# A fused attention and gated-MLP kernel with its Gelu in three stages in place of four (two segments share one stage, two are read from PSUM) and with new scheduling rules

## The chip, the cores and the metric

The kernel runs on one core of one Trainium2 chip. The metric is the device time of one launch in microseconds (us). The kernel before took 312.73 us (median of 3 runs, 310.44 to 313.6) when the prediction was made. The profile is one execution on that core; its span runs from the first to the last instruction and is 1 to 2 us shorter than the time of the same run.

## The reference, cut to what matters

Two branches read the same `x` (2048 tokens, 512 channels) and are mixed by a gate per token. Branch A works in four segments of 512 tokens with 32 heads of width 16: softmax attention inside the segment, plus a linear memory `M, z` that is carried from segment to segment. Branch B is a gated MLP with 1792 hidden channels.

```
for s in range(4):                       # segments of 512 tokens
    p = softmax(q_s k_s^T * scale + mask); a_dot = p v_s
    a_mem = (phi(q_s) M) / (phi(q_s) z + 1e-6)      # phi(t) = t+1 if t>0 else exp(t)
    o_s = g * a_mem + (1 - g) * a_dot
    M += phi(k_s)^T v_s ;  z += sum phi(k_s)
a = concat(o_s) @ wo
b = (gelu(x @ w_gate) * (x @ w_up)) @ w_down
out = sigmoid(x . gate_w) * a + (1 - that) * b
```

Exp and Gelu both run on ScalarE, and the traces show a table load of 1.28 us there at each change from one to the other, so the order of the two on ScalarE matters.

## The kernel before

The kernel is written as tasks with estimated durations; when it is built, a list scheduler in Python puts them in one fixed order per engine. So "the kernel" is a task graph, a set of picking rules, and the order that falls out of them. Every engine is given its own fixed order, with semaphores to wait on in it.

The kernel uses eight banks of PSUM, the memory that its matmuls write to. Four (`X`) hold one fill of attention scores, one (`P`) the result of the probabilities times the values (called PV here), and three (`W`) serve all other matmuls. One exp reads all four score banks at once.

```
# the pick (cut)
for e in ENGINES:
    for t in ready[e]:
        st = max(cur[e], ready_at[t.id])
        if t.tiled == "pv":
            ...                                  # PV goes right after a score fill, else
            st += PATIENCE                       # it is held back by 3 us
        if t.grp is not None and t.grp.bank is None:
            if not bank_free: continue
            st = max(st, min(bank_free.values()))
        k = (st, -t.prio, t.id)
        if best is None or k < best[0]: best = (k, e, t)
```

```
# one fill (cut): scores into X[0..3], one exp of 128x2048, masks on GpSimd;
# five fills and two PVs per group of 8 heads, 20 fills per segment, 80 in all
exp: activation(PT[slot], XALL, Exp, scale=ATT_SCALE)

def gates(s):      # hidden tile ft: 4 matmuls into a W bank, copied out by ScalarE or VectorE
    copy_out(f"Gev{s}_{ft}", g, hT[s%2][:, ft, :], g.f32(), ..., engs=(ACT, DVE))
def gelu(s):       # 14 tiles in 4 chunks, SBUF to SBUF, after all exps of phase s
    ... after=exp_tasks[s] + previous chunk
def ups_down(s):   # 14 x 4 up matmuls, multiplied into hT by VectorE, then 4 tiles of
    ...            # wo (4 matmuls) + wd (14 matmuls), in pieces of 3, attention part first
    ostage[tile % 2] = psum * omgt               # ScalarE or VectorE; two output buffers

prep(0)
for s in range(4):
    attention(s)
    prep(s + 1)            # K, Q, V, gate, phi(q), memory read; phi(k) and memory update
    gates(s); gl = gelu(s); ups_down(s, gl)
```

`prep(s+1)` runs in phase `s`, under the exps of the segment ahead. `hT` has two slots, so hidden states of two segments can be held.

The softmax here doesn't subtract the row's maximum and nothing guards it: scores larger than these inputs give would overflow.

Of the kernel before, what the change touches and what calls it, by code (L numbers as in the profile page):

```python
# [12 lines left out]
ALU = mybir.AluOpType  # L13
# [13 lines left out]
PATIENCE = 3.0  # L27
HOP = {PE: 0.17, ACT: 0.07, DVE: 0.07, POOL: 0.10, SP: 0.0}
# [40 lines left out]
class Task:  # L69


    def __init__(self, name, alts, grp=None, after=(), bias=0.0, nbytes=0):
# [6 lines left out]
        self.tiled = None  # L79
        self.est = {e: sum(i.est for i in l) for e, l in alts.items()}  # L80
# [13 lines left out]
class Sched:  # L94
# [32 lines left out]
    def schedule(self):  # L127
# [6 lines left out]
        for g in groups.values():  # L134
            for t in g[1:]:
                for d in t.preds:
                    if d.grp is not g[0].grp and d is not g[0]:
                        if d not in g[0].preds:
                            g[0].preds.add(d)
                            d.succs.add(g[0])  # L140
# [23 lines left out]
        while len(order) < n:  # L164
            best = None
            for e in ENGINES:
                for t in ready[e]:
                    st = max(cur[e], ready_at[t.id])
                    if t.tiled == "pv":
                        if last_pe == "qk" and ready_at[t.id] <= cur[e]:  # L170
                            best = ((-1.0, 0.0, t.id), e, t)
                            continue
                        st += PATIENCE
# [4 lines left out]
                    k = (st, -t.prio, t.id)  # L178
# [150 lines left out]
def _build(es, nc, A_x, A_wq, A_wk, A_wv, A_wo, A_beta, B_w_gate, B_w_up, B_w_down, gate_w, out):  # L329
# [41 lines left out]
    ostage = [sb(f"ost{i}", [P, 512]) for i in range(2)]  # L371
# [149 lines left out]
    gelu_last = [None] * NSEG  # L521

# [45 lines left out]
    def prep(s):  # L568
# [51 lines left out]
        if s > 0:  # L620
# [14 lines left out]
            for qt in range(4):  # L635
# [14 lines left out]
                    issue=1.25, transpose=True)  # L650
        if s < NSEG - 1:
            for i in range(2):
                phi_task("pk", s, ph, kT, "kT", kT, "kT", i)
# [27 lines left out]
    def attention(s):  # L681
        sl = s % 2
        for t in range(4):
            slots = {}

            def fill(name, steps, diags):
# [4 lines left out]
                for (j, kb, ncol, c0) in steps:  # L691
                    for g in range(4):
# [4 lines left out]
                            [("kpad", j, sl, t), ("qT", sl, t)], [("X", g)], 0.4 * ncol / 512 / 4))  # L697
                task(f"qk{s}_{t}{name}", PE, instrs).tiled = "qk"
# [3 lines left out]
                    [("X", g) for g in range(4)], [("PT", slot)], act_t(2048))], after=after)  # L702
                minstrs = []
# [13 lines left out]
            def pv(j, sa, sbk, sc):  # L717
                i2 = t % 2
                instrs = []
                for kb in range(4):  # L720
                    slot, c0 = ((sa, 0), (sbk, 0), (sc, 256 * j), (sbk, 384))[kb]
                    for q in range(4):
# [5 lines left out]
                            [("PT", slot), ("Vaug", sl, kb)], [("P",)], 0.04))  # L728
                task(f"pv{s}_{t}_{j}", PE, instrs).tiled = "pv"
# [3 lines left out]
            def norm():  # L733
# [9 lines left out]
                          [("recip", i2)], 0.25),  # L743
                    Instr(lambda e: e.tensor_tensor(sc1[i2][:], recip[i2][:], gd, ALU.mult),
                          [("recip", i2), ("GdT", sl)], [("sc1", i2)], 0.2),
                    Instr(lambda e: e.tensor_tensor(ov, tv[:, :, :, 0:16], rb, ALU.mult),  # L746
                          [("Tb", i2, 0), ("Tb", i2, 1), ("sc1", i2)], [("obf", i2)], dve_t(512)),
                    Instr(lambda e: e.transpose(dst, obf[i2][:]), [("obf", i2)], dk, dve_t(512))]  # L748
                if s > 0:
                    ins.append(Instr(lambda e, t=t: e.tensor_tensor(oT[sl][:, t, :], oT[sl][:, t, :], ott[i2][:],  # L750
                                                                    ALU.add), ok + dk, ok, dve_t(512, 2)))
# [11 lines left out]
    CHUNKS = [(0, 2), (2, 6), (6, 10), (10, 14)]  # L763

    def gates(s):
        sl, x3 = s % 2, s % NX
        for ft in range(NFT):
            g = Grp(banks)
            pieces(f"G{s}_{ft}", g, [mm(g, lambda g=g: g.f32()[:, :], wg[:, kb, ft * 128:(ft + 1) * 128],
                                        xT[x3][:, kb, :], [("xT", x3, kb), ("w", ("wg", ft // 7))], kb == 0,  # L770
                                        kb == 3, 512) for kb in range(4)], 2)
            copy_out(f"Gev{s}_{ft}", g, lambda ft=ft: hT[sl][:, ft, :], lambda g=g: g.f32()[:, :], [g.key],
                     [("hT", sl, ft)], 512)

    def gelu(s):
        sl = s % 2
        res = []
        for ci, (f0, f1) in enumerate(CHUNKS):
            hk = [("hT", sl, ft) for ft in range(f0, f1)]
            res.append(task(f"gelu{s}_{ci}", ACT, [Instr(  # L780
                lambda e, f0=f0, f1=f1: e.activation(hT[sl][:, f0:f1, :], hT[sl][:, f0:f1, :],  # L781
# [124 lines left out]
```

## Time and profile before

| | before |
|---|---|
| time, us | 312.73 |
| span of the profiled run, us | 309.8 |
| TensorE / VectorE / ScalarE busy | 90% / 65% / 71% |
| TensorE idle in the span, us | 30.0 |
| 80 exps of 128x2048, each | 1.877 us |
| a warm matmul of 512 columns, one after another | 0.2165 us |

The page's first part has busy time, share of the span and instruction count of each engine:

```profile
PE 279.8 (90%) x2185; PEld 114.1 (37%) x2185; DVE 202.1 (65%) x352; ACT 218.8 (71%) x163; POOL 104.4 (34%) x193
```

The span was cut at the starts of exps number 0, 19, 20, 39, 40, 59, 60 and 79 (counted from 0). The stretch ahead of the first exp (15.4 us) is left out. Rows 1, 3, 5 and 7 are stretches of 19 rounds of "scores, exp", rows 2, 4 and 6 hold a last exp of a phase and the Gelu stage behind it, and the last row runs from the last exp to the end. Columns of the windows view, kernel before: stretch and length; busy time and instruction count of TensorE, weight loads, VectorE, ScalarE and GpSimd; then the granted TensorE clock, the DMA share and GB/s.

```profile
...
15.41:72.87 57.46, 50.30 (x446) 19.59 (x448) 44.91 (x87) 47.72 (x43) 26.64 (x58) 0.97 0.42 117
72.87:84.80 11.93, 11.47 (x95) 5.76 (x88) 10.34 (x18) 11.87 (x9) 1.28 (x2) 1.00 0.22 44
84.80:140.31 55.51, 49.54 (x431) 19.35 (x433) 42.30 (x77) 41.13 (x28) 23.46 (x42) 0.97 0.14 25
140.31:151.27 10.96, 10.96 (x76) 5.21 (x69) 5.07 (x8) 10.90 (x7) 1.27 (x2) 1.00 0.24 48
151.27:206.23 54.96, 50.86 (x443) 20.27 (x444) 42.09 (x71) 42.19 (x31) 23.28 (x42) 1.00 0.02 6
206.23:217.19 10.96, 10.49 (x86) 4.89 (x79) 6.56 (x11) 10.90 (x7) 1.27 (x2) 1.00 0.13 36
217.19:271.33 54.14, 51.91 (x426) 20.26 (x428) 32.59 (x53) 38.02 (x24) 20.02 (x26) 1.00 0.08 19
271.33:309.80 38.47, 33.29 (x177) 14.17 (x169) 16.49 (x26) 11.68 (x9) 1.27 (x2) 1.00 0.06 21
```

The timeline of ScalarE shows the first Gelu stage of before. Columns: start, duration, engine, source line, operation, out<-in and count:

```profile
72.87 1.88 ACT L700 ACTIVATE pt<-psXALL 128x2048 bf16<-128x2048 f32 x1 [0.33 <-PE psXALL L693]
...
75.26 1.28 ACT L781 ACT_TABLE_LOAD   x1
76.55 4.66 ACT L781 ACTIVATE hT<-hT 128x1024 bf16<-128x1024 bf16 x3
...
83.51 1.28 ACT L700 ACT_TABLE_LOAD   x1
84.80 1.88 ACT L700 ACTIVATE pt<-psXALL 128x2048 bf16<-128x2048 f32 x1
```

And the timeline of TensorE at the end of before (L402 is the helper that emits all `W` matmuls):

```profile
275.40 12.75 PE L402 MATMUL psW<-xT,wu 128*128 128x512 bf16 x56
...
288.74 1.47 PE L402 MATMUL psW<-wo,oT 128*128 128x512 bf16 x6
292.27 0.39 PE L402 MATMUL psW<-wo,oT 128*128 128x512 bf16 x1 [2.07 <-DVE oT L750]
...
300.91 5.78 PE L402 MATMUL psW<-wd,hT 128*128 128x512 bf16 x26
```

After the last exp all ups and downs of the last segment are still to do, and one wait of 2.07 us falls among them: the attention part of the down tile needs the last normalised output (`oT`), which VectorE is only just finishing.

### The profile page before, as it was taken

What the parts mean: (1) busy time and instruction counts of PE and PEld (TensorE: products, weight loads), DVE (VectorE), ACT (ScalarE), POOL (GpSimd) and SP (SyncE); (2) the same over time, 40 slices, a digit from 0 to 9 for tenths busy, and PEclk for the clock granted to TensorE, in tenths of its full rate; (3) what the DMA queues carried; (4) which work ended last, traced back from release to release, by engine and by line L of the source; (5) the groups of instructions that cost most, each with busy time, mean ns of one, the idle gap of its engine ahead of it and who ended that gap; (6) DMA issues with size and microseconds to landing.
All of it is one profiled execution on the core that took longest, in us unless ns stands there. A gap on an engine that the chain in (4) does not pass through costs nothing.

```text
span 309.8 us, 5374 instructions
## 1 busy us (share of the span) xinstructions
PE 279.8 (90%) x2185; PEld 114.1 (37%) x2185; DVE 202.1 (65%) x352; ACT 218.8 (71%) x163; POOL 104.4 (34%) x193
## 2 busy tenths in 40 slices
PE   5999779979976997999989997989998999999795
PEld 1434223334422333444424333434432433344242
DVE  0176799688888977394796767846668274657600
ACT  1399679678996876579989867769866677793000
POOL 7036434732033834332065433330334243410000
PEclk9599979999997999999999999999999999999999
DMA  6999600022200000633100000001400000000000
GB/s 202 260 360 300 119 19 0 2 47 47 45 2 0 2 0 1 87 87 67 37 0 2 0 0 2 1 2 51 72 18 2 0 19 17 2 34 0 2 34 34
DMA packets 29769, 15.30 MB, mean 49 GB/s; under 512 B 21296, under 2 KB 29744, under 8 KB 29744
## 3 DMA queue, kind: packets, MB, share of 16 engines
q1 hardware_dynamic: 28160, 13.91, 17.9%
q10 hardware_dynamic: 1584, 1.05, 1.1%
q8 instruction: 17, 0.28, 0.4%
q14 instruction: 8, 0.07, 0.1%
HBM read 8.14 MB, written 2.10 MB: 33 GB/s over the span
## 4 chain that ended last, share of the span: by engine, by line
PE 59%; DVE 18%; SPq 8%; ACT 8%; issue 3%; DMA 2%; POOL 2%; ACTq 0%; DVEq 0%; POOLq 0%
PE psW L402 48%; PE psXALL L693 6%; PE psP L724 5%; ACT pt L700 4%; SPq L433 4%; SPq L429 3%; DVE obf L746 3%; DMA betaT<-in_A_beta_dram 2%; DVE tb L730 2%; DVE oT L750 2%; DVE ott L748 2%; ACT hT L781 2%; DVE hT L419 1%; POOL exsT L611 1%; DVE hT L796 1%
## 5 line engine op out<-in xcount | busy, mean ns | idle before, releaser
L700 ACT ACTIVATE pt<-psXALL 128x2048 bf16<-128x2048 f32 x80 | 150.1, 1877 | 47.3 <-PE psXALL L693 38.9
L711 POOL TENSOR_SCALAR_AFFINE_SELECT pt<-pt 128x512 bf16<-128x512 bf16 (+1 forms) x112 | 83.0, 743 | 165.2 <-ACT pt L700 155.7
L402 PE MATMUL psW<-xT,wg 128*128 128x512 bf16 x224 | 56.3, 386 | 5.3 <-DVE hT L419 3.4
L402 PE MATMUL psW<-xT,wu 128*128 128x512 bf16 x224 | 53.6, 380 | 3.2 <-DVE hT L796 3.1
L402 PE MATMUL psW<-wd,hT 128*128 128x512 bf16 x224 | 54.3, 379 | 0.0
L796 DVE TENSOR_TENSOR hT<-psW,hT 128x512 bf16<-128x512 f32 x56 | 36.6, 685 | 13.5 <-PE psW L402 13.3
L730 DVE STREAM_TRANSPOSE tb<-psP 128x512 f32<-128x512 f32 x32 | 22.9, 715 | 28.5 <-PE psP L724 28.1
L419 DVE CAST hT<-psW 128x512 bf16<-128x512 f32 x41 | 27.6, 684 | 8.9 <-PE psW L402 8.5
L402 PEld LDWEIGHTS psW<-xT,wg 128*128 128x128 bf16 x224 | 19.3, 98 | 32.0 <-DVE hT L419 6.4
L402 PEld LDWEIGHTS psW<-xT,wu 128*128 128x128 bf16 x224 | 19.7, 98 | 30.3 <-DVE hT L796 6.7
L402 PEld LDWEIGHTS psW<-wd,hT 128*128 128x128 bf16 x224 | 21.2, 98 | 24.8 <-issue 1.4
L781 ACT ACTIVATE hT<-hT 128x2048 bf16<-128x2048 bf16 (+1 forms) x16 | 26.0, 1686 | 0.0
L724 PE MATMUL psP<-pt,vaug 128*17 128x256 bf16 (+3 forms) x512 | 24.3, 309 | 1.2 <-POOL pt L711 1.2
L693 PE MATMUL psXALL<-qT,kpad_0 32*128 32x512 bf16 (+3 forms) x256 | 15.8, 301 | 5.6 <-ACT pt L700 4.4
L811 ACT ACTIVATE ost<-psW,omgt 128x512 bf16<-128x512 f32 x5 | 3.4, 686 | 24.6 <-PE psW L402 23.7
L402 PE MATMUL psW<-wo,oT 128*128 128x512 bf16 x64 | 17.5, 381 | 3.5 <-DVE oT L750 2.1
L402 PE MATMUL psW<-xT,wq 128*128 128x512 bf16 x64 | 17.5, 396 | 1.9 <-DVE mzacc L666 1.7
L814 DVE TENSOR_SCALAR ost<-psW,omgt 128x512 bf16<-128x512 f32 x11 | 8.1, 747 | 17.0 <-PE psW L402 17.0
L402 PE MATMUL psW<-xT,wk 128*128 128x512 bf16 x64 | 18.3, 421 | 0.0
L693 PE MATMUL psXALL<-qT,kpad_1 32*128 32x512 bf16 (+3 forms) x256 | 16.0, 304 | 1.9 <-ACT pt L700 1.9
L611 POOL COPY exsT<-exs 32x4 f32<-32x4 f32 x64 | 15.7, 245 | 3.7
L402 PE MATMUL psW<-wv,xT 128*128 128x512 bf16 x64 | 15.6, 380 | 0.0
(83 smaller groups left out, 238.7 us busy)
## 6 DMA issues: line engine op xcount, KB each, us to landing
out_dram<-ost SPq DMA_DIRECT2D x16, 128.0 KB, 1.7
wg<-in_B_w_gate_dram SPq DMA_DIRECT2D x2, 896.0 KB, 7.6
wu<-in_B_w_up_dram SPq DMA_DIRECT2D x2, 896.0 KB, 7.9
wd<-in_B_w_down_dram SPq DMA_DIRECT2D x1, 1792.0 KB, 15.1
wk<-in_A_wk_dram ACTq DMA_DIRECT2D x1, 512.0 KB, 4.3
hT<-in_A_x_dram SPq DMA_DIRECT2D x4, 128.0 KB, 5.0
wq<-in_A_wq_dram ACTq DMA_DIRECT2D x1, 512.0 KB, 6.0
wv<-in_A_wv_dram SPq DMA_DIRECT2D x1, 512.0 KB, 8.2
```

The source lines that it names most:

```text
L402: return Instr(lambda e: e.matmul(view(), lhsT, rhs, start=first, stop=last), reads=reads, writes=[fkey if fkey is not None else g.key], e ...
L419: alts[DVE] = [Instr(lambda e: e.tensor_copy(dst(), src()), reads=reads, writes=writes, est=dve_t(n))]
L429: return e.dma_start_transpose(out_ap(), in_ap())
L433: return e.dma_start(out_ap(), in_ap())
L611: cross = task(f"exsT{s}", POOL, [Instr(lambda e, g=g, c=c: e.tensor_copy(exsT[sl][32 * g:32 * g + 32, c:16:4], exs[32 * c:32 * c + 32, s4 ...
L693: instrs.append(Instr(lambda e, t=t, g=g, j=j, kb=kb, ncol=ncol, c0=c0: e.matmul(X[g][:, c0:c0 + ncol], kpad[j][sl][32 * g:32 * g + 32, t, ...
L700: prev_exp[0] = exp_task(s, f"exp{s}_{t}{name}", [Instr(lambda e: e.activation(PT[slot][:], XALL[:, :].rearrange("p (g c) -> p g c", g=4), ...
L711: minstrs.append(Instr(lambda e, view=view, pat=pat: e.affine_select(out=view, in_=view, compare_op=ALU.is_ge, fill=0.0, base=0, pattern=p ...
L724: instrs.append(Instr(lambda e, q=q, kb=kb, slot=slot, c0=c0, h=h: e.matmul(Pb[32 * q:32 * q + 17, 128 * kb:512], Vaug[sl][:, kb, h, :], P ...
L730: task(f"pvt{s}_{t}_{j}", DVE, [Instr(lambda e: e.transpose(Tb[i2][:, j, :], Pb[:, :]), [("P",)], [("Tb", i2, j)], dve_t(512))])
L781: lambda e, f0=f0, f1=f1: e.activation(hT[sl][:, f0:f1, :], hT[sl][:, f0:f1, :], ACTF.Gelu_apprx_tanh), hk, hk,
L796: task(f"Um{s}_{ft}", DVE, [Instr(lambda e, g=g, ft=ft: e.tensor_tensor(hT[sl][:, ft, :], g.f32()[:, :], hT[sl][:, ft, :], ALU.mult), [g.k ...
```

## The change

The intent: spend one table switch less inside the kernel, spare half the copies of gate results, move the last Gelu ahead of the last attention so that TensorE has work beside the last exps, and stop the scheduler from putting copies on ScalarE where an exp could start. The diff, cut to its core; cuts are marked:

```diff
+OPEN_BONUS = 6.0
 ...
+            due = min([ready_at[t.id] for t in ready[ACT] if t.tiled == "exp"] + [1e9])
             for e in ENGINES:
                 for t in ready[e]:
                     st = max(cur[e], ready_at[t.id])
+                    if e == ACT and t.tiled != "exp" and st + t.est[e] > due + 0.1:
+                        continue
 ...
-                        st += PATIENCE
+                        st += t.patience          # 3.0; 0.0 for a segment's last PV
 ...
-                    k = (st, -t.prio, t.id)
+                    open_ = t.grp is not None and t.grp.bank is not None
+                    k = (st, -t.prio - (OPEN_BONUS if open_ else 0.0), t.id)
 ...
-                for d in t.preds:                 # first matmul of a group inherits the
+                for d in () if t.ahead or PE in t.alts else t.preds:  # reader's needs
 ...                                               # (estimates of norm, fills, PV raised)
-    def gelu(s): ...                              # SBUF chunks, one stage per segment
+    def gelu_phase(p, copied, direct):
+        for s, chunks in copied: ...              # as before, larger chunks
+        for s in direct:
+            for ft in range(NFT):
+                g = gate_mms(s, ft)
+                t = task(f"gelu{s}_{ft}", ACT, [activation(hT[s%2][:, ft, :], g.f32(), Gelu)],
+                         after=exp_tasks[p] + prev)
+                t.ahead = True
+                # first gate matmul of ft=0 comes after the last score fill of phase p
 ...
-            pieces(f"D{s}_{tile}", g, ins, 3, after=dep)
+            seq = dwn + att if last else att + dwn     # last segment: attention part last
+            # last tile of all goes into the free score bank X[0]
+            pieces(f"D{s}_{tile}", g, ins, 2, after=dep)
+            f.ahead = True                        # 4 output buffers in place of 2
 ...
+    prep(0); memory(0); attention(0); xdma(2); prep(1)
+    gates_copied(0); gates_copied(1)
+    gelu_phase(0, [(0, (2, 4, 4, 4)), (1, (7, 7))], [])
+    memory(1); attention(1); ups(0); downs(0); xdma(3); prep(2)
+    gelu_phase(1, [], [2])
+    memory(2); attention(2); ups(1); downs(1); prep(3)
+    gelu_phase(2, [], [3])
+    attention(3); ups(2); downs(2); ups(3); downs(3)
```

`memory(s)` (phi of the keys, its transposition by DMA, the sums for `M` and `z`) was the end of `prep(s)`; it now comes one phase later.

More of the change, by code (lines that the diff above doesn't have):

```diff
@@ L79, in __init__ @@
         self.tiled = None
+        self.patience = 0.0
+        self.ahead = False
         self.est = {e: sum(i.est for i in l) for e, l in alts.items()}
@@ L135, in schedule @@
             for t in g[1:]:
-                for d in t.preds:
-                    if d.grp is not g[0].grp and d is not g[0]:
-                        if d not in g[0].preds:
-                            g[0].preds.add(d)
-                            d.succs.add(g[0])
+                for d in () if t.ahead or PE in t.alts else t.preds:
+                    if d.grp is not g[0].grp and d not in g[0].preds:
+                        g[0].preds.add(d)
+                        d.succs.add(g[0])
         indeg = [len(t.preds) for t in tasks]
@@ L370, in _build @@
     sc1 = [sb(f"sc1_{i}", [P, 2, 16], F32) for i in range(2)]
-    ostage = [sb(f"ost{i}", [P, 512]) for i in range(2)]
+    ostage = [sb(f"ost{i}", [P, 512]) for i in range(4)]
     wq = sb("wq", [P, 4, 512])
@@ L521, in _build @@
     gelu_last = [None] * NSEG
+    last_qk = [None] * NSEG
     def exp_task(phase, name, instrs, **kw):
@@ L650, in prep, with memory @@
                     issue=1.25, transpose=True)
+    def memory(s):
+        sl = s % 2
         if s < NSEG - 1:
             for i in range(2):
-                phi_task("pk", s, ph, kT, "kT", kT, "kT", i)
+                phi_task("pk", s, s, kT, "kT", kT, "kT", i)
             for t in range(4):
@@ L696, in fill @@
                             tile_position=(32 * g, 0)),
-                            [("kpad", j, sl, t), ("qT", sl, t)], [("X", g)], 0.4 * ncol / 512 / 4))
-                task(f"qk{s}_{t}{name}", PE, instrs).tiled = "qk"
+                            [("kpad", j, sl, t), ("qT", sl, t)], [("X", g)], 0.425 * ncol / 512 / 4))
+                last_qk[s] = task(f"qk{s}_{t}{name}", PE, instrs)
+                last_qk[s].tiled = "qk"
                 after = [prev_exp[0]] if prev_exp[0] is not None else []
@@ L702, in fill @@
                     [("X", g) for g in range(4)], [("PT", slot)], act_t(2048))], after=after)
+                prev_exp[0].tiled = "exp"
                 minstrs = []
@@ L727, in pv @@
                             tile_position=(0, 32 * q)),
-                            [("PT", slot), ("Vaug", sl, kb)], [("P",)], 0.04))
-                task(f"pv{s}_{t}_{j}", PE, instrs).tiled = "pv"
+                            [("PT", slot), ("Vaug", sl, kb)], [("P",)], 0.043))
+                p = task(f"pv{s}_{t}_{j}", PE, instrs)
+                p.tiled = "pv"
+                p.patience = 0.0 if (t, j) == (3, 1) else PATIENCE
                 task(f"pvt{s}_{t}_{j}", DVE, [Instr(lambda e: e.transpose(Tb[i2][:, j, :], Pb[:, :]),
@@ L742, in norm @@
                     Instr(lambda e: e.reciprocal(recip[i2][:], tv[:, :, :, 16]), [("Tb", i2, 0), ("Tb", i2, 1)],
-                          [("recip", i2)], 0.25),
+                          [("recip", i2)], 0.35),
                     Instr(lambda e: e.tensor_tensor(sc1[i2][:], recip[i2][:], gd, ALU.mult),
-                          [("recip", i2), ("GdT", sl)], [("sc1", i2)], 0.2),
+                          [("recip", i2), ("GdT", sl)], [("sc1", i2)], 0.34),
                     Instr(lambda e: e.tensor_tensor(ov, tv[:, :, :, 0:16], rb, ALU.mult),
-                          [("Tb", i2, 0), ("Tb", i2, 1), ("sc1", i2)], [("obf", i2)], dve_t(512)),
+                          [("Tb", i2, 0), ("Tb", i2, 1), ("sc1", i2)], [("obf", i2)], 0.79),
                     Instr(lambda e: e.transpose(dst, obf[i2][:]), [("obf", i2)], dk, dve_t(512))]
@@ L750, in norm @@
                     ins.append(Instr(lambda e, t=t: e.tensor_tensor(oT[sl][:, t, :], oT[sl][:, t, :], ott[i2][:],
-                                                                    ALU.add), ok + dk, ok, dve_t(512, 2)))
+                                                                    ALU.add), ok + dk, ok, 0.7))
                 task(f"norm{s}_{t}", DVE, ins)
@@ L761, in attention, with gate_mms, gates_copied, ups @@
             norm()
-    CHUNKS = [(0, 2), (2, 6), (6, 10), (10, 14)]
-    def gates(s):
+    gelu_of = {}
+    def gate_mms(s, ft):
+        g = Grp(banks)
+        x3 = s % NX
+        pieces(f"G{s}_{ft}", g, [mm(g, lambda: g.f32()[:, :], wg[:, kb, ft * 128:(ft + 1) * 128], xT[x3][:, kb, :],
+                                    [("xT", x3, kb), ("w", ("wg", ft // 7))], kb == 0, kb == 3, 512)
+                                 for kb in range(4)], 2)
+        return g
+    def gates_copied(s):
+        for ft in range(NFT):
+            g = gate_mms(s, ft)
+            copy_out(f"Gev{s}_{ft}", g, lambda ft=ft: hT[s % 2][:, ft, :], lambda g=g: g.f32()[:, :], [g.key],
+                     [("hT", s % 2, ft)], 512)
+    def gelu_phase(p, copied, direct):
+        prev = []
+        for s, chunks in copied:
+            f0 = 0
+            for n in chunks:
+                hk = [("hT", s % 2, ft) for ft in range(f0, f0 + n)]
+                hv = hT[s % 2][:, f0:f0 + n, :]
+                t = task(f"gelu{s}_{f0}", ACT, [Instr(lambda e, hv=hv: e.activation(hv, hv, ACTF.Gelu_apprx_tanh),
+                                                     hk, hk, act_t(512 * n, False) + (0.0 if prev else 1.3))],
+                         after=exp_tasks[p] + prev)
+                prev = [t]
+                for ft in range(f0, f0 + n):
+                    gelu_of[s, ft] = t
+                f0 += n
+        for s in direct:
+            for ft in range(NFT):
+                g = gate_mms(s, ft)
+                t = task(f"gelu{s}_{ft}", ACT, [Instr(
+                    lambda e, g=g, ft=ft, s=s: e.activation(hT[s % 2][:, ft, :], g.f32()[:, :],
+                                                            ACTF.Gelu_apprx_tanh),
+                    [g.key], [("hT", s % 2, ft)], act_t(512) + (0.0 if prev else 1.3))], grp=g,
+                    after=exp_tasks[p] + prev)
+                t.ahead = True
+                mine = [x for x in S.tasks if x.grp is g and x is not t]
+                lead = last_qk[p] if ft == 0 else lead
+                mine[0].preds.add(lead)
+                lead.succs.add(mine[0])
+                lead = mine[-1]
+                prev = [t]
+                gelu_of[s, ft] = t
+        gelu_last[p] = prev[0]
+    def ups(s):
         sl, x3 = s % 2, s % NX
@@ L768, in gates @@
             g = Grp(banks)
-            pieces(f"G{s}_{ft}", g, [mm(g, lambda g=g: g.f32()[:, :], wg[:, kb, ft * 128:(ft + 1) * 128],
-                                        xT[x3][:, kb, :], [("xT", x3, kb), ("w", ("wg", ft // 7))], kb == 0,
-                                        kb == 3, 512) for kb in range(4)], 2)
-            copy_out(f"Gev{s}_{ft}", g, lambda ft=ft: hT[sl][:, ft, :], lambda g=g: g.f32()[:, :], [g.key],
-                     [("hT", sl, ft)], 512)
-    def gelu(s):
-        sl = s % 2
-        res = []
-        for ci, (f0, f1) in enumerate(CHUNKS):
-            hk = [("hT", sl, ft) for ft in range(f0, f1)]
-            res.append(task(f"gelu{s}_{ci}", ACT, [Instr(
-                lambda e, f0=f0, f1=f1: e.activation(hT[sl][:, f0:f1, :], hT[sl][:, f0:f1, :],
-                                                     ACTF.Gelu_apprx_tanh), hk, hk,
-                act_t(512 * (f1 - f0), False) + (1.3 if ci == 0 else 0.0))],
-                after=exp_tasks[s] + (res[-1:] if res else [])))
-        gelu_last[s] = res[-1]
-        return res
-    def ups_down(s, gl):
-        sl, x3 = s % 2, s % NX
-        for ft in range(NFT):
-            ci = [i for i, (a, b) in enumerate(CHUNKS) if a <= ft < b][0]
-            g = Grp(banks)
             pieces(f"U{s}_{ft}", g, [mm(g, lambda g=g: g.f32()[:, :], wu[:, kb, ft * 128:(ft + 1) * 128],
                                         xT[x3][:, kb, :], [("xT", x3, kb), ("w", ("wu", ft // 7))], kb == 0,
-                                        kb == 3, 512) for kb in range(4)], 2, after=[gl[ci]])
+                                        kb == 3, 512) for kb in range(4)], 2, after=[gelu_of[s, ft]])
             task(f"Um{s}_{ft}", DVE, [Instr(lambda e, g=g, ft=ft: e.tensor_tensor(
@@ L798, in ups_down, with downs @@
                 [("hT", sl, ft)], dve_t(512))], grp=g)
+    def downs(s):
+        sl = s % 2
+        last = s == NSEG - 1
+        hdep = [S._w[("hT", sl, fb)] for fb in range(NFT)]
         for tile in range(4):
             gt = 4 * s + tile
-            g = Grp(banks)
-            ins = [mm(g, lambda g=g: g.f32()[:, :], oT[sl][:, kb, tile * 128:(tile + 1) * 128], wo[:, kb, :],
-                      [("oT", sl, tile, kb), ("w", "wo")], kb == 0, False, 512) for kb in range(4)]
-            ins += [mm(g, lambda g=g: g.f32()[:, :], hT[sl][:, fb, tile * 128:(tile + 1) * 128], wd[:, fb, :],
-                       [("hT", sl, fb), ("w", "wd")], False, fb == NFT - 1, 512) for fb in range(NFT)]
@@ L806, in ups_down @@
-            dep = [S._w[("hT", sl, fb)] for fb in range(NFT)] + [S._w[("oT", sl, tile, 3)]]
-            pieces(f"D{s}_{tile}", g, ins, 3, after=dep)
-            i2 = tile % 2
-            rd = [g.key, ("omgt", s)]
-            S.add(Task(f"fin{s}_{tile}", {
-                ACT: [Instr(lambda e, g=g, gt=gt, i2=i2: e.activation(ostage[i2][:], g.f32()[:, :], ACTF.Copy,
-                                                                      scale=omgt[:, gt:gt + 1]), rd,
-                            [("ost", i2)], act_t(512, ap=True))],
-                DVE: [Instr(lambda e, g=g, gt=gt, i2=i2: e.tensor_scalar(ostage[i2][:], g.f32()[:, :],
-                                                                         omgt[:, gt:gt + 1], None, ALU.mult), rd,
-                            [("ost", i2)], dve_t(512, ap=True))]}, grp=g))
@@ L817, in ups_down @@
-            dma(f"out{gt}", SP, lambda gt=gt: out[0, gt * 128:(gt + 1) * 128, :], lambda i2=i2: ostage[i2][:],
-                [("ost", i2)], [("hbm", gt)], 131072, sm=sem_out[gt])
+            on_x = last and tile == 3
+            g = None if on_x else Grp(banks)
+            key = ("X", 0) if on_x else g.key
+            view = (lambda: X[0]) if on_x else (lambda g=g: g.f32()[:, :])
+            att = [(oT[sl][:, kb, tile * 128:(tile + 1) * 128], wo[:, kb, :], [("oT", sl, tile, kb), ("w", "wo")])
+                   for kb in range(4)]
@@ new lines, in downs @@
+            dwn = [(hT[sl][:, fb, tile * 128:(tile + 1) * 128], wd[:, fb, :], [("hT", sl, fb), ("w", "wd")])
+                   for fb in range(NFT)]
+            seq = dwn + att if last else att + dwn
+            ins = [mm(g, view, a, b, rd, i == 0, i == len(seq) - 1, 512, fkey=key)
+                   for i, (a, b, rd) in enumerate(seq)]
+            dep = hdep + (fins if last else [S._w[("oT", sl, tile, 3)]])
+            pieces(f"D{s}_{tile}", g, ins, 2, after=dep)
+            rd = [key, ("omgt", s)]
@@ new lines, in downs @@
+            f = S.add(Task(f"fin{s}_{tile}", {
+                ACT: [Instr(lambda e, view=view, gt=gt, tile=tile: e.activation(
+                    ostage[tile][:], view(), ACTF.Copy, scale=omgt[:, gt:gt + 1]), rd, [("ost", tile)],
+                    act_t(512, ap=True))],
+                DVE: [Instr(lambda e, view=view, gt=gt, tile=tile: e.tensor_scalar(
+                    ostage[tile][:], view(), omgt[:, gt:gt + 1], None, ALU.mult), rd, [("ost", tile)],
+                    dve_t(512, ap=True))]}, grp=g))
@@ L820, in _build @@
+            f.ahead = True
+            if s == NSEG - 2:
+                fins.append(f)
+            dma(f"out{gt}", SP, lambda gt=gt: out[0, gt * 128:(gt + 1) * 128, :],
+                lambda tile=tile: ostage[tile][:], [("ost", tile)], [("hbm", gt)], 131072, sm=sem_out[gt])
+    fins = []
     sem_out = [sem("so") for _ in range(16)]
     prep(0)
-    for s in range(NSEG):
-        attention(s)
-        if s + 2 < NSEG:
-            xdma(s + 2)
-        if s + 1 < NSEG:
-            prep(s + 1)
-        gates(s)
-        gl = gelu(s)
-        ups_down(s, gl)
+    memory(0)
@@ L832, in _build @@
+    attention(0)
+    xdma(2)
+    prep(1)
+    gates_copied(0)
+    gates_copied(1)
+    gelu_phase(0, [(0, (2, 4, 4, 4)), (1, (7, 7))], [])
+    memory(1)
+    attention(1)
+    ups(0)
+    downs(0)
+    xdma(3)
+    prep(2)
+    gelu_phase(1, [], [2])
+    memory(2)
+    attention(2)
+    ups(1)
+    downs(1)
+    prep(3)
+    gelu_phase(2, [], [3])
+    attention(3)
+    ups(2)
+    downs(2)
+    ups(3)
+    downs(3)
     for t in S.schedule():
```

## The prediction

> **What bounds the kernel now.** The busy table: TensorE 90% of a 309.8 us span, ScalarE 71%, VectorE 65%. Two loops interlock. (a) The 80 exponentials of 128x2048 (1.88 us each): the four score banks are single-buffered, so the timeline shows scores, exp, scores, exp, at best 2.6 us a round. (b) TensorE: in the timeline 8 projection matmuls take 1.83 and 10 take 2.27 us, so 0.2165 each (the Trainium skill, "TensorE: Matmul & The Clock Gate", section "Wait — 56ns, not 53.3ns?", gives 215.7 ns warm at N=512; the trace agrees); a score fill takes 0.33, a PV group 0.65. From the first fill at 14.8 us this sums to about 262 us: a floor near 280 us. The chain of waits gives TensorE 59%, VectorE 18%, ScalarE 8%. The ScalarE timeline has the four Gelu stages (about 9 us each with two table loads of 1.28) at 75, 142, 208 and 273 us. After the last exp (273 us) come 36 us of almost pure TensorE work, with 5 us of TensorE idle.
>
> **What the change does.** The instruction order shows the same matmuls. Gates of segments 0 and 1 are copied early and Gelu'd in one stage between exps 20 and 21 (about 17 us); segments 2 and 3 are Gelu'd from PSUM, 14 times 0.55 us, after exps 40 and 60. Hidden-state copies fall from 56 to 28 (41 to 20 on VectorE): 14 us of VectorE off. Table loads fall from 8 to 7. The work after the last score fill falls from 145 to 76 matmuls of 512 columns, 31.4 to 16.5 us, because ups and downs of segments 2 and 3 fill the last exps. The price: exps 20 to 79 are later, by a longer Gelu stage and fuller rounds.
>
> **Costing.** For every round I took the larger of TensorE's sum and the exp round. For before this ends TensorE at 291.6 us; the trace has 306.8. The missing 15 are waits on VectorE results and half-clock spells near 40 and 93 us. The new order gives 284.5: TensorE idle by that reckoning falls from 14.5 to 8.4. Corrections: the first fill has 4 matmuls more ahead of it, still slow: +1.5; phase 0 stays VectorE-tight (about 50 us of VectorE work in 54): +5; direct Gelu stages, whose gate matmuls wait for three banks: +2.5 each; exps 60 to 79 +1.5; tail +1; final copy and store +3. Span about 301, time about 302. Nearly all the gain is on the critical path: TensorE idle filled, and fewer VectorE waits.
>
> **Predicted: 302 us, 80% range 295 to 309. Faster by over 2%: 0.76; within 2%: 0.21; slower by over 2%: 0.03.**
>
> **What would show it.** TensorE work after the last exp about 18 us rather than 36; last exp near 280 us instead of 271; exp 21 near 90 us (before 84.8); direct Gelu stages about 13 us with TensorE near full; TensorE busy 93%; VectorE busy about 187 us; ScalarE about the same (217).
>
> **What would make it wrong.** VectorE saturating in phase 0, where all 28 copies meet the next segment's projections: +5 more. The 17 us Gelu stage leaving TensorE idle about 3 us and its clock halved after. Direct Gelu stages locked to ScalarE by three banks, 1 us a tile rather than 0.87. The other way: better VectorE estimates in the scheduler could remove more of the 15 us than I allow, towards 295.

## The result

The changed kernel takes 298.28 us (median of 4 runs, 297.99 to 300.09); before, in the same session, 312.05 (310.44 to 313.6). The ratio is 0.9571, with a 95% interval of 0.9506 to 0.9636. All ratios here are the mean time of one kernel's fast runs over that of the other's of the same rounds, so they are not quite the ratio of the medians.

The page's first part, kernel after:

```profile
PE 277.6 (94%) x2185; PEld 115.2 (39%) x2185; DVE 193.1 (65%) x335; ACT 215.6 (73%) x169; POOL 102.5 (35%) x193
```

The span is 296.6 us. The windows of after, cut at the same exps, same columns (the stretch ahead of the first exp, 15.2 us, is left out again):

```profile
...
15.22:66.90 51.68, 51.07 (x435) 20.47 (x437) 43.38 (x81) 43.88 (x38) 25.96 (x58) 1.00 0.46 121
66.90:84.99 18.09, 16.10 (x137) 7.90 (x130) 16.59 (x30) 18.03 (x12) 1.27 (x2) 1.00 0.14 30
84.99:137.36 52.37, 48.80 (x437) 20.09 (x439) 38.48 (x69) 41.90 (x30) 23.83 (x42) 0.98 0.14 34
137.36:155.28 17.92, 17.92 (x105) 7.67 (x98) 5.78 (x10) 12.80 (x17) 1.27 (x2) 0.88 0.08 16
155.28:208.44 53.16, 49.95 (x441) 20.35 (x442) 39.47 (x67) 41.93 (x30) 22.59 (x42) 1.00 0.09 23
208.44:224.12 15.68, 15.28 (x110) 7.10 (x103) 7.07 (x13) 12.58 (x17) 1.27 (x2) 1.00 0.01 2
224.12:275.85 51.73, 49.36 (x400) 19.21 (x401) 33.52 (x52) 35.66 (x20) 19.12 (x26) 1.00 0.09 22
275.85:296.60 20.75, 17.73 (x108) 7.70 (x100) 5.53 (x10) 3.94 (x4) 1.27 (x2) 1.00 0.08 26
```

Sum the two tables by kind of stretch:

| stretch | before, us | after, us | difference |
|---|---|---|---|
| start to the first exp | 15.4 | 15.2 | -0.2 |
| four times 19 rounds | 222.1 | 208.9 | -13.1 |
| three Gelu stages between exps | 33.9 | 51.7 | +17.8 |
| last exp to the end | 38.5 | 20.8 | -17.7 |

(The differences are taken before rounding.) This is the main reading. The end is 17.7 us shorter, the Gelu stages are 17.8 us longer: the work moved and nothing was won by moving it alone. By place, the whole gain is in the rounds, at 2.75 us each in place of 2.92. As span less busy time, TensorE idles 19.0 us in place of 30.0; 6.6 of these 11.0 us are in the first row, the first 19 rounds. The remaining 2.2 us of the span are less busy time for the same 2185 matmuls. Read the table as where time went missing, not as its cause: mem_old below has a first stretch of 57.3 us again and is not shown to be slower than after.

The waits view tells which waits went: added up over the whole trace, TensorE's waits for VectorE fall from 14.7 to 7.2 us, those for ScalarE from 7.4 to 5.9. The two largest for VectorE before, and the largest after (who waited, line, for whom; total, times, longest; L796 and L834 are the same line, where VectorE multiplies the ups into `hT`, and L419 is the copy helper):

```profile
PE psW L402 <- DVE hT L796: 5.1, 4, 1.6
PE psW L402 <- DVE hT L419: 3.4, 3, 2.7
```

```profile
PE psW L408 <- DVE hT L834: 2.6, 3, 1.6
```

The timeline of ScalarE, kernel after, in the first stage that reads Gelu from PSUM:

```profile
137.36 1.88 ACT L711 ACTIVATE pt<-psXALL 128x2048 bf16<-128x2048 f32 x1 [1.52 <-PE psXALL L703]
139.25 1.28 ACT L813 ACT_TABLE_LOAD   x1
140.55 0.60 ACT L813 ACTIVATE hT<-psW 128x512 bf16<-128x512 f32 x1
...
145.60 0.60 ACT L813 ACTIVATE hT<-psW 128x512 bf16<-128x512 f32 x1 [0.27 <-PE psW L408]
146.46 0.60 ACT L813 ACTIVATE hT<-psW 128x512 bf16<-128x512 f32 x1 [0.27 <-PE psW L408]
...
153.99 1.28 ACT L711 ACT_TABLE_LOAD   x1
155.28 1.88 ACT L711 ACTIVATE pt<-psXALL 128x2048 bf16<-128x2048 f32 x1
```

One Gelu every 0.86 us, of which ScalarE works 0.60 and waits 0.27 for TensorE: four matmuls of 0.2165 us are 0.866. From here on the stage is bound by TensorE, not by ScalarE and not by the three banks. (Its first gates were slower, in a spell of half clock that is shown below.)

The timeline of TensorE at the end, kernel after:

```profile
277.12 3.19 PE L408 MATMUL psW<-wd,hT 128*128 128x512 bf16 x14
...
280.66 0.72 PE L736 MATMUL psP<-pt,vaug 128*17 128x512 bf16 x16
281.32 3.20 PE L408 MATMUL psW<-wd,hT 128*128 128x512 bf16 x14
...
284.78 3.19 PE L408 MATMUL psW<-wd,hT 128*128 128x512 bf16 x14
287.80 1.89 PE L408 MATMUL psW<-wo,oT 128*128 128x512 bf16 x8
```

The ups are gone from here, and three times 14 `wd` matmuls now come ahead of the attention parts that need the last `oT`. There is no wait where before had 2.07 us.

### The profile page after: what moved, and what is told of

Its sections match the earlier page's. It is cut to its first block, busy times and chain, and to the rows that moved or that the text cites. A ratio compares the mean times of both kernels' runs of the same rounds, so it can differ in the third digit from the quotient of the medians.

```text
span 296.6 us, 5371 instructions
## 1 busy us (share of the span) xinstructions
PE 277.6 (94%) x2185; PEld 115.2 (39%) x2185; DVE 193.1 (65%) x335; ACT 215.6 (73%) x169; POOL 102.5 (35%) x193
## 4 chain that ended last, share of the span: by engine, by line
PE 74%; ACT 11%; DVE 9%; DMA 2%; issue 2%; SPq 0%; POOL 0%; ACTq 0%; DVEq 0%
PE psW L408 59%; PE psXALL L703 8%; PE psP L736 6%; ACT pt L711 5%; ACT hT L802 3%; DMA hT<-in_A_x_dram 2%; PE psXALL L408 1%; ACT L711 1%; DVE vaug L425 1%; DVE hT L834 1%; DVE kpad_0 L582 1%; DVE kT L425 1%; DVE tb L744 1%; DVE obf L760 1%; DVE kpad_1 L590 1%
## 5 line engine op out<-in xcount | busy, mean ns | idle before, releaser
L408 PE MATMUL psW<-xT,wg 128*128 128x512 bf16 x224 | 53.0, 389 | 0.0
L408 PE MATMUL psW<-wd,hT 128*128 128x512 bf16 x210 | 50.7, 380 | 0.0
L834 DVE TENSOR_TENSOR hT<-psW,hT 128x512 bf16<-128x512 f32 x56 | 37.7, 686 | 8.6 <-PE psW L408 8.0
L408 PEld LDWEIGHTS psW<-xT,wg 128*128 128x128 bf16 x224 | 21.0, 100 | 27.2 <-issue 4.9
L408 PEld LDWEIGHTS psW<-wd,hT 128*128 128x128 bf16 x210 | 18.9, 97 | 23.7 <-issue 3.6
L813 ACT ACTIVATE hT<-psW 128x512 bf16<-128x512 f32 x28 | 16.5, 597 | 8.1 <-PE psW L408 8.1
L408 PE MATMUL psW<-xT,wk 128*128 128x512 bf16 x64 | 17.0, 395 | 0.1
L650 DVE TENSOR_TENSOR otok<-psW,ndsc 128x512 bf16<-128x512 f32 x12 | 7.6, 683 | 13.2 <-PE psW L408 13.1
L408 PE MATMUL psW<-wo,oT 128*128 128x512 bf16 x60 | 15.8, 380 | 0.0
L736 PEld LDWEIGHTS psP<-pt,vaug 128*17 128x17 bf16 x512 | 10.1, 90 | 13.4 <-issue 6.6
L425 DVE CAST hT<-psW 128x512 bf16<-128x512 f32 x20 | 13.2, 676 | 2.6 <-PE psW L408 2.6
```

The lines of the kernel that those rows point to most:

```text
L408: return Instr(lambda e: e.matmul(view(), lhsT, rhs, start=first, stop=last), reads=reads, writes=[fkey if fkey is not None else g.key], e ...
L425: alts[DVE] = [Instr(lambda e: e.tensor_copy(dst(), src()), reads=reads, writes=writes, est=dve_t(n))]
L650: Instr(lambda e, gn=gn, qt=qt: e.tensor_tensor(otok[:, qt, :].rearrange("p (h e) -> p h e", e=16), gn.f32()[:, :].rearrange("p (h e) -> p ...
L736: instrs.append(Instr(lambda e, q=q, kb=kb, slot=slot, c0=c0, h=h: e.matmul(Pb[32 * q:32 * q + 17, 128 * kb:512], Vaug[sl][:, kb, h, :], P ...
L813: lambda e, g=g, ft=ft, s=s: e.activation(hT[s % 2][:, ft, :], g.f32()[:, :], ACTF.Gelu_apprx_tanh),
L834: task(f"Um{s}_{ft}", DVE, [Instr(lambda e, g=g, ft=ft: e.tensor_tensor(hT[sl][:, ft, :], g.f32()[:, :], hT[sl][:, ft, :], ALU.mult), [g.k ...
```

## The experiments

Twelve kernels ran, in three sessions of four. Each ratio is against the kernel before on the same chip in the same session (medians 311.78, 311.65 and 311.64 us). Differences between kernels of different sessions are differences of such ratios. All results were correct.

| kernel | time, us | ratio (95%) | exps 0 to 19, us | last exp to end, us |
|---|---|---|---|---|
| before | 312.05 | 1 | 57.5 | 38.5 |
| after | 298.28 | 0.9571 (0.9506-0.9636) | 51.7 | 20.8 |
| rules_only | 308.87 | 0.9885 (0.9846-0.9923) | 57.5 | 36.5 |
| old_rules | 310.24 | 0.9955 (0.9909-1.0) | 55.6 | 22.4 |
| late_gelu3 | 299.91 | 0.9612 (0.9582-0.9642) | 51.7 | 36.0 |
| all_copied | 296.73 | 0.9513 (0.9476-0.9551) | 51.7 | 27.7 |
| four_stages | 305.38 | 0.9790 (0.9748-0.9832) | 52.2 | 43.2 |
| no_due | 301.03 | 0.9661 (0.9624-0.9699) | 58.1 | 14.1 |
| no_bonus | 305.49 | 0.9795 (0.9755-0.9836) | 53.3 | 28.4 |
| old_est | 300.69 | 0.9651 (0.9618-0.9684) | 52.2 | 20.7 |
| copy2_direct3 | 295.89 | 0.9498 (0.9464-0.9533) | 52.8 | 25.1 |
| mem_old | 300.08 | 0.9605 (0.9573-0.9637) | 57.3 | 20.8 |
| copied_mem_old | 299.44 | 0.9596 (0.9564-0.9629) | 54.1 | 27.6 |
| old_downs | 309.30 | 0.9914 (0.9885-0.9942) | 51.7 | 27.6 |

Two theories stood at the start. R: the scheduler's rules bring the gain. S: the new order of gates, Gelu and downs brings it.

### rules_only and old_rules: is it the rules or the structure?

```diff
 # rules_only: the kernel before, plus
+ exp-due rule, OPEN_BONUS = 6.0, group predecessors, last PV without patience, new estimates
 # old_rules: the kernel after, minus
- exp-due rule;  OPEN_BONUS = 0.0;  patience 3 for every PV;  old estimates
```

> The kernel before with the scheduler's new rules alone (no ScalarE copy where an exp falls due, preference for open PSUM groups, corrected VectorE and TensorE estimates, group predecessors, patience of the last PV); gates, four Gelu stages and the order of ups and downs as before. Theory R (rules): most of the 13.8 us come from the rules, so 302 us or less. Theory S (structure): the new order of gates, Gelu and downs brings them, so 309 or more. My own guess lies between, 305: the first 20 rounds should go from 57.5 us (before) to about 53, the tail after the last exp stays near 36 us.

> The kernel after with the old rules: no exp-due rule, no preference for open groups, old estimates, patience 3 for all PV. The rule on group predecessors stays, as the Gelu from PSUM needs it. Theory R: 308 us or more. Theory S: 301 or less. My guess 304: first 20 rounds about 57 us rather than 51.7, tail after the last exp about 20.

Measured: 308.87 and 310.24 us. Each theory fails on one of them: the rules alone bring 1.2%, the structure alone 0.5% (its interval reaches 1.0, so this may be nothing), both together 4.3%. The rule on group predecessors is in both kernels and was never taken out alone, and "structure" here takes in the moved memory update and the new output stage. My guesses in between (305 and 304) were wrong too, because I had taken the two parts as adding up. In rules_only the first 19 rounds stayed at 57.5 us; I had expected 53. In old_rules the end did become short (22.4 us) and nearly nothing was gained by it.

### late_gelu3: is the short end the source of the gain?

```diff
-    gelu_phase(2, [], [3])
+    gelu_last[2] = gelu_last[1]
     attention(3)
+    gates_copied(3)
     ups(2)
     downs(2)
+    gelu_phase(3, [(3, (2, 4, 4, 4))], [])
```

> The kernel after, but segment 3's gates copied during its own attention and its Gelu done from SBUF after the last exp, as before (the third stage moves to the end). If filling the last exps with the ups and downs of segment 3 is a main source of the gain, this loses 5 us or more (303 or above), tail back from 20.7 to about 34 us with the last exp only 10 us earlier. If only TensorE idle counts and the copies fit, it stays within 3 us of after (under 301.5).

Measured: 299.91 us, ratio 0.9612. From the last exp to the end it again takes 36.0 us, almost as in before, and yet the kernel is within 1.6 us of after, and the intervals overlap. The last exp simply starts earlier, at 262.1 us rather than 275.9. Filling the last exps is not where the gain comes from.

### all_copied and copy2_direct3: is Gelu straight from PSUM worth it?

```diff
 # all_copied (copy2_direct3: only the first of the two)
-    gelu_phase(1, [], [2])
+    gates_copied(2)
+    gelu_phase(1, [(2, (2, 4, 4, 4))], [])
-    gelu_phase(2, [], [3])
+    gates_copied(3)
+    gelu_phase(2, [(3, (2, 4, 4, 4))], [])
```

> The kernel after with Gelu of segments 2 and 3 from copies in SBUF too (stages of about 9 us), same three places. If reading straight from PSUM is worth its change: 28 more copies (19 us on VectorE or ScalarE) cost 3 us or more, 301 or above. If the two direct stages (17.9 and 15.7 us from exp to exp) were a real loss, this is 2 us or more faster than after, 296 or below. If only TensorE's total counts, within 2 us of 298.3.

> The kernel after with segment 2's Gelu from copies and only segment 3's straight from PSUM. In after, TensorE idles 3.5 us in the rounds just ahead of segment 2's direct stage, because its gate matmuls may not start before the last score fill; ahead of segment 3's it idles about 1 us. If that idling is what all_copied saves (1.6 us), this equals all_copied, ratio 0.951 to 0.953. If each direct stage costs the same by itself, it lies halfway, about 0.954 to 0.955; if it is segment 3's that costs, it equals after, 0.957.

Measured: 296.73 us (0.9513) and 295.89 us (0.9498). The 28 copies more did not cost the 3 us expected: VectorE is busy 202.3 us in place of 193.1 and still has slack. By the medians both are 1.5 to 2.4 us faster than after, but they come from other sessions and the intervals overlap, so "not slower" is what is shown. copy2_direct3, with the lowest time of all, is not shown to differ from all_copied, which points to segment 2's stage as the place of what there may be to win. There the trace of after has a visible fault. Its gate matmuls may not start before the last score fill, so nothing fills the rounds ahead of it. Windows of after, same columns as above:

```profile
132.00:134.00 2.00, 0.42 (x5) 0.10 (x4) 1.90 (x4) 1.36 (x2) 0.68 (x2) 1.00 0.00 0
134.00:136.00 2.00, 0.58 (x4) 0.34 (x4) 1.96 (x3) 1.84 (x1) 0.58 (x2) 0.74 0.00 0
...
138.00:140.00 2.00, 2.00 (x17) 0.62 (x6) 0.72 (x1) 1.98 (x2) 0.64 (x1) 0.50 0.64 130
```

TensorE works 1.0 us of 4, and from about 135.0 to 141.8 its clock is half. The Trainium skill ("TensorE: Matmul & The Clock Gate", Part 1, "What's actually happening") says that the clock is halved after at least one idle window of about 3.4 us; the 0.50 agrees with the half rate, the idle window does not, as no single wait here was longer than 1.65 us. But the spell is not shown to cost time: two of after's four runs had a mean granted clock of 0.994 rather than the profiled run's 0.983, so hardly had such a spell, and took 297.99 and 298.26 us against 298.30. (The stage that holds it does look longer: 17.92 us, where segment 3's, at full clock, takes 15.68.) The idling ahead of it, 3 us of 4, is what remains as the likely cost. In the trace of all_copied there is no such spell (clock 0.994).

### four_stages: are the early gates needed?

```diff
-    gates_copied(0); gates_copied(1)
-    gelu_phase(0, [(0, (2, 4, 4, 4)), (1, (7, 7))], [])
+    gates_copied(0)
+    gelu_phase(0, [(0, (2, 4, 4, 4))], [])          # and so on: each segment's gates in its
+    ...                                             # own phase, fourth stage at the end
```

> The kernel after (all its rules, memory update moved, tail details) but with four Gelu stages as before, each segment's gates copied in its own phase. Theory E: the gain needs the gates of segment 1 early, as matmuls that are ready in phase 0 when TensorE would wait; then this is 306 us or more, with 35 us or more after the last exp. Rival: the rules with the moved memory update are enough, then 301 or less. I expect about 307: by sums of rounds TensorE idle is 15 us here and 8 in after.

Measured: 305.38 us, ratio 0.9790, 2.2 points above after. So gates of segment 1 in phase 0, with the Gelu stage that they share with segment 0, are needed for half of the gain, and my guess of 307 was near. The run also takes Gelu of segments 2 and 3 from copies and puts the last stage at the end, but all_copied and late_gelu3 show little cost of either. The early gates and the fourth stage itself were not separated. The first 19 rounds are as quick as after's (52.2 us); the loss is in the next 19 (55.4 us against 52.4) and at the end (43.2). My reading, argued and not shown by itself, is that the early gates are a store: TensorE fills the rounds of phase 0 with gates, and what is then left for later, ups and downs, fills the later rounds.

### no_due, no_bonus, old_est: which rule?

```diff
 # no_due
-            due = min(...)
-                    if e == ACT and t.tiled != "exp" and st + t.est[e] > due + 0.1: continue
 # no_bonus
-OPEN_BONUS = 6.0
+OPEN_BONUS = 0.0
 # old_est: recip 0.25, scale 0.2, product 0.69, sum 0.42 again in place of 0.35, 0.34, 0.79, 0.7;
 # fills 0.4 in place of 0.425, PV 0.04 a matmul in place of 0.043
```

> The kernel after without the rule that holds a ScalarE copy back when an exp falls due. If this rule carries the gain of the rules (old rules 310, after 298): 306 or more, with more ScalarE copies and longer rounds in phase 0. If it is not the rule: 301 or less. My guess 302.

> The kernel after without the preference for groups whose PSUM bank is already taken. If this carries the rules' gain: 306 or more, as three banks are held by half-done groups and VectorE gets its tiles late. If not: 301 or less. My guess 305: sums of rounds give 6 us more TensorE idle.

> The kernel after with the old estimates (normalisation of the attention output put at 2.4 us in place of 3.2 on VectorE, fills and PV 6% shorter). If the estimates carry the rules' gain: 306 or more, TensorE waiting on VectorE over 30 us rather than 20. If not: 301 or less. My guess 301.

Measured, as points of ratio above after's 0.9571: the exp-due rule 0.9, the preference for open groups 2.2, the estimates 0.8. (The estimate of a whole normalisation falls from 2.87 to 2.25 us; the expectation's 3.2 and 2.4 were added up wrongly.) Only the second is clear of noise: the intervals of no_due and old_est overlap after's. The three sum to 3.9, and old_rules, which drops all three and the patience of the last PV, is 3.8 above. That agrees with rules that add up among themselves, and the preference for groups that already hold a bank would be more than half. In the first 19 rounds of no_bonus weight loads wait 5.1 us for VectorE, in after 1.2 us. The wait that makes the difference, no_bonus and then after:

```profile
PEld psW L408 <- DVE hT L425: 4.1, 6, 2.0
```

```profile
PEld psW L408 <- DVE hT L425: 0.2, 1, 0.2
```

That half-done groups sit on the three banks is how I explain it; no run shows the banks themselves.

The exp-due rule is in the change's stated intent, but it is a small part at most. Without it ScalarE makes 50.3 us of work in the first 19 rounds in place of 43.9, the rounds stretch to 58.1 us, and the end shrinks to 14.1 us.

### mem_old and copied_mem_old: does the place of the memory update matter?

```diff
 def memory(s):
-    phi_task("pk", s, s, ...)
+    phi_task("pk", s, max(s - 1, 0), ...)
 ...
     prep(1)
+    memory(1)
 ...                     # memory(2) likewise after prep(2); both removed from their new places
```

> The kernel after with the memory update (exp and sums of the keys, state matmuls) put back where before has it: inside the phase in which the segment's keys are projected, ahead of the next attention. If moving it was part of the gain (rules_only and four_stages differ by 1% with this move and the tail details between them): 300.5 us or more, ratio 0.965 or above. If not: within 1% of after, 0.948 to 0.964. My guess 0.957; by sums of rounds TensorE idle is 0.7 us less.

> A version meant to beat both: all Gelu from copies, memory update at its old place. By sums of rounds TensorE idle is 1.6 us less than in all_copied. If the sums hold: about 295 us, ratio 0.946; if the extra VectorE work in phase 0 takes it back: 297 or more, 0.952 or above.

Measured: 0.9605 and 0.9596. For mem_old the difference from after (0.3 points) is not resolved. But copied_mem_old, which I meant as a version to beat both, is 2.7 us slower than all_copied, against an expectation of 1.6 us faster: the intervals (0.9564-0.9629 and 0.9476-0.9551) do not overlap. Sums of rounds do not see what happens. The first 19 rounds of mem_old take 57.3 us, as in before. Its waits, listed as engine, line, who was waited for, total, times and longest:

```profile
DVE kT L425 <- DMA phkt<-kT: 4.8, 3, 3.4
...
PE psW L408 <- DVE kT L425: 3.4, 1, 3.4
```

`kT` has one buffer. phi(k) is formed in it and transposed out of it by DMA, and only then may the next segment's K be copied in. With the memory update of segment 1 due in phase 0, its K is projected early and meets that DMA: VectorE waits, the `W` bank stays taken, and TensorE, whose order is fixed, waits 3.4 us behind it; the 8 gate matmuls that follow take 3.60 us, at a clock of 0.50. With the update a phase later the K projections come late in phase 0 (at 62.3 us in after, at 32.1 in mem_old), where the transposition is long done. rules_only, with the update at its old place too, shows the same wait (3.0 us) and a first stretch of 57.5 us.

The kernel before doesn't show this wait in its first 19 rounds, though it has the update there. TensorE's longest waits there are for exps that free the score banks:

```profile
PE psXALL L693 <- ACT pt L700: 4.2, 4, 2.3
```

Much of the loss comes back later, too: mem_old's first 19 rounds are 5.6 us longer than after's, its span only 2.3 us.

### old_downs: do the details of the output stage matter?

```diff
-    ostage = [... for i in range(4)]
+    ostage = [... for i in range(2)]
-    on_x = last and tile == 3;  seq = dwn + att if last else att + dwn
+    on_x = False;               seq = att + dwn
-    dep = hdep + (fins if last else ...);  pieces(..., 2, after=dep);  f.ahead = True
+    dep = hdep + ...;                      pieces(..., 3, after=dep);  f.ahead = False
```

> The kernel after with the output stage of before: two output buffers, down groups that wait for their buffer, pieces of three, attention part first also in the last segment, no spare score bank for the last tile. If these details are part of the gain: 301 us or more (ratio 0.966 or above), with the time from the last exp to the end 2 us longer or TensorE waits before it. If not: within 1.5 us of after. My guess 301.5, as sums of rounds give 3.6 us more TensorE idle.

Measured: 309.30 us, ratio 0.9914. I had guessed 301.5; these details, not in the change's description, are needed for 3.4 of its 4.3%. Of 11.9 us in the span, 6.9 are at the end (27.6 us after the last exp's start in place of 20.8). Its TensorE timeline:

```profile
282.27 0.59 PE L736 MATMUL psP<-pt,vaug 128*17 128x512 bf16 x4 [0.92 <-DVE tb L744]
284.23 0.82 PE L736 MATMUL psP<-pt,vaug 128*17 128x384 bf16 x12 [1.37 <-POOL pt L723]
284.98 1.46 PE L408 MATMUL psW<-wo,oT 128*128 128x512 bf16 x3
288.42 0.61 PE L408 MATMUL psW<-wo,oT 128*128 128x512 bf16 x1 [1.98 <-DVE oT L764]
288.82 5.04 PE L408 MATMUL psW<-wd,hT 128*128 128x512 bf16 x14
```

Once ups and downs have been moved ahead, nothing is left to cover the last masks, the last PV and the last normalisation: three waits stand bare (0.92, 1.37, 1.98 us), and after them 14 `wd` matmuls take 5.04 us instead of 3.19. The windows of old_downs show the clock at half (it fell at about 282.4 us, after waits of 1.15, 1.15 and 0.92 us):

```profile
286.00:288.00 2.00, 0.44 (x2) 0.00 (x0) 1.86 (x5) 0.00 (x0) 0.00 (x0) 0.50 0.00 0
...
290.00:292.00 2.00, 2.00 (x6) 0.76 (x5) 0.00 (x0) 0.00 (x0) 0.00 (x0) 0.50 0.00 0
```

Here the halved clock does cost: 14 matmuls 1.85 us. The change has the `wd` matmuls of three tiles as cover, ahead of the attention parts, and shows neither the waits nor the half clock there. As span less busy time old_downs idles 25.6 us (19.0 in after), and its matmuls are busy 5.3 us longer. The other 5.0 us are lost before the last exp; whether to two buffers, to groups that wait for their buffer, or to pieces of three, was not separated.

## Why the prediction was right, and where it was not

The time (302 predicted, 295 to 309; 298.28 measured) and the direction were right. Point by point:

- **What bounds the kernel: right.** Two interlocked loops, with TensorE's total as the floor. Among kernels with complete matmul records the span goes roughly with TensorE's idle time: 30.0 us (before), 29.1 (old_rules), 26.7 (rules_only), 19.0 (after), 18.7 (all_copied), for spans of 309.8, 307.9, 309.2, 296.6 and 294.2. Only roughly, as busy time differs too, by up to 7 us: old_downs idles 25.6 us, less than rules_only, in a span of 308.5.
- **Signs named ahead: mostly right.** After the end of the last exp 18.9 us remain (20.75 less the exp's 1.88; "about 18" predicted, 36.6 before). TensorE is busy 94% (93% predicted), ScalarE 215.6 us (217), VectorE 193.1 (187). Direct stages advance at 0.86 us a tile, as for 0.87 predicted.
- **"phase 0 stays VectorE-tight: +5" and "the first fill ... +1.5": wrong.** These were the failing terms. The first exp starts at 15.2 us, as in before, and 19 rounds take 51.7 us where the bare sum of rounds gave 51.4 (my working; redone from the order in after's trace it gives 51.6). So the last exp came at 275.9 us, not near 280, and exp 20 (the prediction's "exp 21") at 85.0, not 90. VectorE was indeed 84% busy there (43.38 of 51.68 us), but TensorE hardly waited for it (0.3 us, and 1.2 us in weight loads). The prediction took the losses of phase 0 in before over to the new order. With the memory update back in phase 0 the new order does lose them: 57.3 us in mem_old, with the wait for a DMA and a single buffer. I had not seen in the diff that moving `memory` takes these off that phase. That before's own losses there came from the same wait is not shown: its trace has other waits (4.2 us for exps).
- **"direct Gelu stages ... +2.5 each": right in sum, by another cause.** Against the sums, exp 40 is 7.1 us late where exp 39 was 1.2 us late; 2.4 us are made up again in the next round, so 3.5 remain. The second direct stage costs 3.7 less 1.9, so 1.8 us; together 5.3, for 5 predicted. The stages wait for their own gate matmuls at TensorE's pace, which the sums had left out, and in the first of them the half clock adds to it (12 gates take 4.47 us, 2.76 in the second). No wait for banks shows in the steady part. That the total fits is luck in part.
- **"Nearly all the gain is on the critical path: TensorE idle filled, and fewer VectorE waits": right, but placed wrongly.** TensorE idles 11.0 us less, and its waits for VectorE fall by 7.5 us. The prediction's account of the change lay on the work moved off the end. late_gelu3 moves it back and loses 1.6 us, which is not resolved. The end's 17.7 us are paid back in the Gelu stages (17.8).
- **The rules were underrated.** The time came out 3.7 us under the forecast, on the side that it had named for better estimates. I listed better estimates as a possible extra. The rules as a whole are needed for 3.8 of the 4.3 points, and none of my sums named the preference for open groups, worth 2.2. (What is needed for the gain adds up to more than the gain: 3.8 for the rules, 3.4 for the output stage, 2.2 for the early gates with their stage. They work together, and no share is any part's own.)
- **Still open:** how much of old_downs' 5.0 us before the last exp belongs to which detail; whether the structure would do with the preference for open groups alone; and whether copy2_direct3 really beats after, which needs both in one session.

## What to carry to other kernels

Where a kernel is bound by the sum of one engine's work, as here, moving work from the end to the middle may win little by itself (late_gelu3: 0.4 points, not resolved): account for the idle time of that engine, stretch by stretch, and ask which wait goes away. Work that is moved away was also cover: here the last normalisation stood bare until the order inside the down tiles was changed with it. In a kernel with a list scheduler the picking rules and the task graph act together (1.2% and 0.5% alone, 4.3% together), so try them together before dropping either, and look at single buffers that a DMA must leave before an engine with a fixed order can go on, because sums of work don't show them.

## What the Trainium skill lacked or had wrong

- "TensorE: Matmul & The Clock Gate", Part 1, "What's actually happening": the page gives an idle window of about 3.4 us as what halves the clock. Here no single wait was that long: in after the clock fell to 0.50 at about 135.0 us, in the second of two waits of 1.35 and 1.65 us, with 0.4 us of work in the 3 us before, and stayed there for about 6.8 us; in old_downs it fell after waits of 1.15, 1.15 and 0.92 us with work between. Low activity was enough. (Of this the page says only, in "A second HAM failure mode: psum-queue depth-cycling", that frequent short idling can make the clock go to and fro, without a length or a share.)
- "ScalarE: Activation LUTs", "What ACT_TABLE_LOAD costs": the page counts 1283 ns for the load plus about 1380 ns of drain for each switch. The load agrees (1.28 us), but no drain shows in these traces: the last exp ends at 139.24 us, the load starts at 139.25 and the Gelu at 140.55, so a switch costs 1.3 us.
- No page says which of several matmul groups to serve first where PSUM banks are few. Preferring the group that already holds a bank was worth 2.2 points here with three banks (no_bonus against after).
